# A new order of the first loads, transposes copied by one engine, and a new priority table in a one-core attention and FFN kernel

## Chip, cores, metric

One core of a Trainium2 chip. The metric is device time of one execution in microseconds (us). "Span" is the profiled length from the first to the last instruction, 1.7 to 1.8 us shorter than the time of the same execution.

## The reference

Layer norm of x (2048 x 512), then x plus two branches: a dilated sliding-window attention (32 heads of 16, window of 8 with step 2) and a gated FFN (512 to 1376 to 512).

```python
x = A_x
xn = _layernorm(x, axis=-1)
return x + _A_ref(xn, A_wqkv, A_wo) + _B_ref(xn, B_w_gate, B_w_up, B_w_down)
# _A_ref: qkv = xn @ wqkv; logits of q with k at pos, pos-2, ... pos-14; softmax; weighted v; @ wo
# _B_ref: (gelu(xn @ w_gate) * (xn @ w_up)) @ w_down
```

## The kernel before

The kernel builds a graph of several hundred tasks. A list scheduler inside the kernel file puts them in one fixed order per engine, from a priority per task, a table of shifts per group of tasks (SHIFT), and constants (SCHED: slack, tolerance). On the chip each engine executes its list strictly in that order, with semaphore waits.

The work goes in four blocks of 512 rows. At the start everything waits for memory, so the first block is done in four tiles of 128 rows: load, statistics, norm (VectorE, with the square root on ScalarE), four transposes on TensorE into PSUM, a copy to SBUF, then Q and K of this tile (16 matmuls of 128 columns each).

```python
# loads: all from the SyncE queue; lower priority value is issued first
prio=(-958, -957.5, -898)[i]                                    # Wq, Wk, Wv: 512 KiB (524 KB) each
prio=((-960, -959), (-957.8, -956.5))[p][t2]                    # tiles 0,1,2,3: 128 KiB (131 KB) each
# -> tile 0, tile 1, Wq, tile 2, Wk, tile 3, Wv

# first tile's transposes lie in two PSUM buffers: ScalarE copies one half, VectorE the other
it_t2 = Item("tpy" + nm, P_ps, "tp") if nm == "0_0" else it_tp
...
# fixed orders within engines
chain(["bnst0", "bnag0", "sub0", "rstd0", "norm0", "bnst1", "bnag1", "evy0_0", "sub1", "rstd1", "norm1",
       "bnst2", ... "norm3", "bnst4"])                           # VectorE; evy0_0 is its half copy
chain(... ["tpx0_0"] + ... + ["mmt0_0", "tpx0_1", "mmt1_0", "mmt0_1", "tpx1_0", "mmt1_1", "tpx1_1",
       "mmt0_2", "mmt1_2", "mmt0_3", "mmt1_3"])                  # TensorE; mmt0_t is Q, mmt1_t is K of tile t
```

After that comes the body: V of the first block, gate and up projections, logits and value products (VectorE multiplies, small TensorE reductions), softmax, later blocks' QKV, output tiles. The gate weight's load waits for Wk's landing; its issue is therefore a clock for that landing.

Of the kernel before, what the change touches and what calls it, by code (L numbers as in the profile page):

```python
# [11 lines left out]
    TOL=dict(pe=0.6, act=-0.3, dve=0.0, pool=0.0, sp=0.0),  # L12
    DMA_ISSUE=0.48,
    DMA_FIXED=2.0,
    DMA_BPUS=330e3,
    ACT_SWITCH=1.35,
    PE_SLACK=0.0,
# [128 lines left out]
class Graph:  # L146
# [466 lines left out]
    def report(self):  # L613
# [11 lines left out]


SHIFT = {
    "acc0": 361, "acc1": -284, "acc3": -893, "er1": 381, "er2": 159, "er3": -18, "ffn0": 449, "ffn1": -216,
    "ffn2": 73, "ffn3": -40, "fin0": -21, "fin1": 305, "fin2": 27, "fin3": -492, "h0": -6, "h1": -944,
    "h2": 606, "ldb1": 326, "ldb2": -35, "ln1": -1581, "ln2": 55, "prod0": 440, "prod1": 888, "prod3": -18,  # L630
    "pv1": -412, "pv2": 970, "pvr0": -976, "pvr1": 126, "pvr2": 463, "qkv1": -43, "qkv2": -1147, "qkv3": -216,
    "sm1": -57, "sm2": -519, "sm3": 750,
}
SCHED = dict(PE_SLACK=1.6, DMA_BPUS=250e3,
             TOL=dict(pe=0.6, act=-0.3, dve=-0.3, pool=-0.3, sp=0.0))

GROUPS = ((r"(?:bnst|bnag|ve|sq|rstd|sub|norm)(\d+)$", "ln", 4), (r"trx(\d+)", "ln", 2),
          (r"(?:mm|evq|evk|evv|stv)(\d)_", "qkv", 1), (r"pr(\d)_", "prod", 1), (r"er(\d)_", "er", 1),
# [21 lines left out]
def d_dve(n, rate=1.04):  # L660
    return 0.07 + n * rate * 1e-3
# [6 lines left out]
def bass_parallel_sum__sliding_local_dilated__glu_gated_geglu__prompt_kernel(nc, A_x, A_wqkv, A_wo, B_x, B_w_gate, B_w_up, B_w_down, out, dbg=None, cfg=None):  # L668
# [41 lines left out]
    with contextlib.ExitStack() as es:  # L710
# [11 lines left out]
        xnT = sb("xnT", [128, NXT, 4, 512], BF)  # L722
# [188 lines left out]
        for p in range(NP):  # L911
# [5 lines left out]
            if p < 2:  # L917
                for t2 in range(2):
                    def mk_ld(t2=t2, p=p, it=it_x):
                        return lambda e: e.dma_start(  # L920
                            XIN[:, it.slot, t2, :], x2[256 * p + 128 * t2:256 * p + 128 * t2 + 128, :])
                    t_x = G.task("sp", "ld_x%d_%d" % (p, t2), 0, mk_ld(), wr=[(it_x, t2)],
                                 prio=((-960, -959), (-957.8, -956.5))[p][t2], nbytes=128 * 1024)
            else:
                def mk_ld(p=p, it=it_x):
                    return lambda e: e.dma_start(
                        XIN[:, it.slot, :, :], x2[256 * p:256 * p + 256, :].rearrange("(t q) d -> q t d", q=128))
                t_x = G.task("sp", "ld_x%d" % p, 0, mk_ld(), wr=[(it_x, 0), (it_x, 1)],
                             prio=(0, 0, -897.5, -897)[p] if p < 4 else -950 + p * 20, nbytes=256 * 1024)
# [77 lines left out]
            for grp in ((0,), (1,)):  # L1007
                n = len(grp)
                nm = "%d_%d" % (p, grp[0])
                it_tp = Item("tpx" + nm, P_ps, "tp")  # L1010
                it_t2 = Item("tpy" + nm, P_ps, "tp") if nm == "0_0" else it_tp

                def mk_tp(it=it_tp, it2=it_t2, ito=it_x, grp=grp, n=n):
                    def f(e):
                        ins = None
                        for q, t2 in enumerate(grp):
                            for kt in range(4):
                                c0 = 1024 * (it, it2)[kt // 2].slot + kt * 128 * n + q * 128
                                ins = e.transpose(PSB[:, c0:c0 + 128], XIN[:, ito.slot, t2, kt * 128:(kt + 1) * 128],
                                                  ident[:, :])  # L1020
                        return ins
                    return f
                t_tp = G.task("pe", "tpx" + nm, d_mm(128, 4 * n), mk_tp(), rd=[(it_x, t2) for t2 in grp] + [I_ident],
                       wr=[it_tp] if it_t2 is it_tp else [it_tp, it_t2], prio=(-200 if b == 0 else base + 4), mode="f", util=0.5)

                t_tp.urgent = b == 0

                o = 256 * (p % 2) + 128 * grp[0]
                if p == 0 and grp[0] == 0:
                    def mk_ev2(it=it_t2, itx=XTI[b], o=o):  # L1030
                        return lambda e: e.tensor_copy(
                            out=xnT[:, itx.slot, 2:4, o:o + 128],
                            in_=PSB[:, 1024 * it.slot + 256:1024 * it.slot + 512].rearrange("q (k c) -> q k c", k=2))
                    t_of["evy" + nm] = G.task("dve", "evy" + nm, d_dve(256), mk_ev2(), rd=[it_t2],
                                              wr=[(XTI[b], ("y", p % 2, grp[0]))], prio=-200)
                nk = 2 if "evy" + nm in t_of else 4

                def mk_ev(it=it_tp, itx=XTI[b], n=n, o=o, nk=nk):
                    return lambda e: e.activation(
                        out=xnT[:, itx.slot, 0:nk, o:o + 128 * n],  # L1040
                        in_=PSB[:, 1024 * it.slot:1024 * it.slot + 128 * nk * n].rearrange("q (k c) -> q k c", k=nk),
                        func=ACTF.Identity)
                t_ev = G.task("act", "evx" + nm, d_act(128 * nk * n), mk_ev(), rd=[it_tp],
                              wr=[(XTI[b], (p % 2, t2)) for t2 in grp], prio=(-200 if b == 0 else base + 6))
                t_of["evx" + nm] = t_ev
                t_of["tpx" + nm] = t_tp
        def chain(names):
            ts = [t_of[q] if isinstance(q, str) else q for q in names]
            for q0, q1 in zip(ts, ts[1:]):
                G.order_after(q1, q0)  # L1050

        chain(["bnst0", "bnag0", "sub0", "rstd0", "norm0", "bnst1", "bnag1", "evy0_0", "sub1", "rstd1", "norm1",
               "bnst2", "bnag2", "sub2", "rstd2", "norm2", "bnst3", "bnag3", "sub3", "rstd3", "norm3", "bnst4"])
        chain(["norm3", "bnst5"])
        chain(["evx0_0", "sq1"])

        QTI = []
        for b in range(NB):
# [7 lines left out]
            if b == 0:  # L1066
                lead = []
                for t in range(4):
                    for which in range(2):
                        it_mm = Item("mmt%d_%d" % (which, t), P_ps, "qkv")  # L1070

                        def mk_mm(which=which, t=t, it=it_mm, itx=XTI[0]):
                            def f(e):
                                ins = None
                                for g in range(4):
                                    for kt in range(4):
                                        ins = e.matmul(  # L1077
                                            PS[:, 512 * it.slot + 128 * g:512 * it.slot + 128 * g + 128],
                                            lhsT=Wqkv[:, kt, which * 512 + g * 128:which * 512 + (g + 1) * 128],
                                            rhs=xnT[:, itx.slot, kt, t * 128:(t + 1) * 128],  # L1080
                                            start=(kt == 0), stop=(kt == 3))
                                return ins
                            return f
                        t_mm = G.task("pe", "mmt%d_%d" % (which, t), 16 * 0.0563, mk_mm(),
                                      rd=[(XTI[0], (t // 2, t % 2)), (I_wq, "qk"[which])]
                                      + ([(XTI[0], ("y", 0, 0))] if t == 0 else []), wr=[it_mm],
                                      prio=-100 + t, mode="f")
                        t_mm.urgent = True
                        t_of["mmt%d_%d" % (which, t)] = t_mm

                        def mk_e(which=which, t=t, it=it_mm, itq=it_qt):
                            def f(e):
                                if which == 0:
                                    o = QT[:, itq.slot, :, t * 128:(t + 1) * 128]
                                else:
                                    o = KT[:, KTI[0].slot, :, 16 + t * 128:16 + (t + 1) * 128]
                                return e.activation(
                                    out=o, in_=PS[:, 512 * it.slot:512 * it.slot + 512].rearrange(
                                        "q (g c) -> q g c", g=4), func=ACTF.Identity)
                            return f  # L1100
                        t_of["ev%s0_%d" % ("qk"[which], t)] = G.task("act", "ev%s0_%d" % ("qk"[which], t), d_act(512), mk_e(), rd=[it_mm],
                               wr=[(it_qt, ("t", t)) if which == 0 else (KTI[0], ("t", t))], prio=-100 + t)
                chain(["evk0_0", "sq3"])
                chain(warm_tasks[:len(WARM[0])] + ["tpx0_0"] + warm_tasks[len(WARM[0]):] +
                      ["mmt0_0", "tpx0_1", "mmt1_0", "mmt0_1", "tpx1_0", "mmt1_1", "tpx1_1",
                       "mmt0_2", "mmt1_2", "mmt0_3", "mmt1_3"])
            for hf in range(nh):
                xparts = [XTI[b]] if nh == 1 else [(XTI[b], (hf, 0)), (XTI[b], (hf, 1))]
                hb = base + (10 * hf if nh > 1 else 0)
# [414 lines left out]
```

## Time and profile before

| | before |
|---|---|
| median time | 196.71 us (3 runs), 196.53 with the run made beside the changed kernel |
| span of the profiled run | 194.6 us |
| TensorE busy | 97% |
| VectorE, ScalarE busy | 79%, 53% |
| first Q / first K matmuls begin; V begins | 6.04 / 7.83; 14.70 us |
| last matmul ends | 192.14 us |

The lines stand in the prediction below. The way to read them: a busy share of 97% says which engine sets the end, not that it is dense. So count matmuls by their spacing, and look for what is left. Three times are read from the chain of waits: where V begins (the end of the last K matmul; the prediction counts from the first V matmul in the chain, 0.05 us later), where the last matmul ends, and the difference. The first is "the start", the difference is "the body".

In the profile lines `PS` is a PSUM buffer, `XIN` a tile of x, `xnT` its transposed norm. L937 is a tile's statistics, L993 the end of its norm, L1019 its transposes on TensorE. The line numbers below differ by 6 or 7 between the kernels: L1077 before is L1071 in the changed kernel (Q and K of the first block), L1123 is L1116 (V, later Q, K, V), L1039 is L1032 (ScalarE's copy), L1308 is L1301 (value products on VectorE), L1329 is L1322 (their reductions on TensorE), L1360 is L1353 (gate and up), L1435 and L1439 are L1428 and L1432 (output tiles). In e5b L1077 is L1078.

### The profile page before, as it was taken

The page shows a single profiled execution, that of the slowest core. Times are in us where ns is not written, and L with a number is a line of the kernel's source. Part 1 is how long each engine was busy: PE and PEld are TensorE (multiplying, and loading weights), DVE is VectorE, ACT ScalarE, POOL GpSimd, SP SyncE. Part 2 cuts the span into 40 slices and gives each one's busy share as a digit, 9 for nine tenths or more (in the row PEclk, how much of TensorE's full clock was granted, in tenths as well). Part 3 has the DMA queues.
Part 4 walks back from the last instruction along what each step waited for, and adds up shares of the span by engine and source line. Part 5 has one row for each costly group of instructions (what it writes and reads, how often), then busy time and mean ns, then how long its engine had stood idle before and what let it go on. Part 6 is the DMA issues. An engine that isn't in the chain of part 4 may idle for free.

```text
span 194.6 us, 3228 instructions
## 1 busy us (share of the span) xinstructions
PE 188.5 (97%) x1205; PEld 91.1 (47%) x1224; DVE 153.6 (79%) x240; ACT 104.1 (53%) x171; POOL 8.5 (4%) x31
## 2 busy tenths in 40 slices
PE   7899999999999999999999999999999999999994
PEld 2794444444444443444434444444444444344484
DVE  5989978999799999998999866998974619972132
ACT  3577583776973679701457701764679006586000
POOL 6011001001000000001000100000000000000000
DMA  5999998998723853063657454014970440010121
GB/s 141 352 398 315 312 169 183 263 193 208 185 57 82 220 141 83 18 167 106 162 157 195 58 136 135 27 45 123 245 185 3 108 136 27 0 59 0 44 77 40
DMA packets 34799, 27.03 MB, mean 139 GB/s; under 512 B 11264, under 2 KB 33248, under 8 KB 34784
## 3 DMA queue, kind: packets, MB, share of 16 engines
q1 hardware_dynamic: 34784, 26.83, 54.1%
q8 instruction: 9, 0.15, 0.4%
q14 instruction: 6, 0.05, 0.1%
HBM read 19.99 MB, written 5.26 MB: 130 GB/s over the span
## 4 chain that ended last, share of the span: by engine, by line
PE 81%; DVE 8%; issue 3%; ACT 3%; DMA 3%; SPq 1%; DVEq 0%; ACTq 0%
PE PS L1360 29%; PE PS L1439 19%; PE PS L1123 13%; PE PS L1435 7%; DVE UNI L1308 4%; PE PS L1329 3%; PE PS L1077 3%; PE PS L1207 3%; DMA Wqkv<-in_A_wqkv_dram 3%; PE PS L1395 1%; DVE UNI L1177 1%; ACT UU L1377 1%; PE PS L1200 1%; DVE HT L1382 1%; DVE HT L1410 1%
## 5 line engine op out<-in xcount | busy, mean ns | idle before, releaser
L1439 PE MATMUL PS<-Wd,HT 128*128 128x512 bf16 (+2 forms) x205 | 40.8, 345 | 0.2
L1360 PE MATMUL PS<-xnT,Wu 128*128 128x512 bf16 x154 | 39.6, 379 | 0.6 <-issue 0.5
L1360 PE MATMUL PS<-xnT,Wg 128*128 128x512 bf16 x156 | 39.4, 379 | 0.4 <-issue 0.3
L1308 DVE TENSOR_TENSOR UNI<-BS,PT 128x2048 bf16<-128x2048 bf16 x32 | 37.1, 1219 | 2.9 <-DMA XR<-in_A_x_dram 1.8
L1177 DVE TENSOR_TENSOR UNI<-QT,KT 128x2048 bf16<-128x2048 bf16 x32 | 37.1, 1218 | 0.2
L1377 ACT ACTIVATE UU<-PS 128x512 bf16<-128x512 f32 x40 | 24.0, 601 | 21.2 <-PE PS L1360 21.1
L1123 PE MATMUL PS<-xnT,Wqkv 128*128 128x512 bf16 x155 | 34.8, 379 | 0.5 <-DVE PS L1245 0.2
L1370 ACT ACTIVATE GG<-PS 128x512 bf16<-128x512 f32 x40 | 23.8, 602 | 18.2 <-PE PS L1360 18.1
L1439 PEld LDWEIGHTS PS<-Wd,HT 128*128 128x128 bf16 x209 | 19.6, 98 | 18.5
L1459 DVE TENSOR_TENSOR OB<-PS,XR 128x512 bf16<-128x512 f32 (+2 forms) x19 | 11.5, 605 | 18.3 <-PE PS L1439 18.3
L1360 PEld LDWEIGHTS PS<-xnT,Wg 128*128 128x128 bf16 x160 | 15.3, 98 | 19.6 <-ACT UU L1377 0.8
L1360 PEld LDWEIGHTS PS<-xnT,Wu 128*128 128x128 bf16 x160 | 15.3, 98 | 19.6 <-issue 0.8
L1123 PEld LDWEIGHTS PS<-xnT,Wqkv 128*128 128x128 bf16 x160 | 15.4, 98 | 19.2 <-issue 0.8
L1382 DVE TENSOR_TENSOR HT<-GG,UU 128x512 bf16<-128x512 bf16 x40 | 15.8, 421 | 9.5 <-ACT UU L1377 9.4
L1435 PE MATMUL PS<-Wo,OT 128*128 128x512 bf16 (+2 forms) x76 | 16.9, 345 | 0.1
L1133 ACT ACTIVATE QT<-PS 128x512 bf16<-128x512 f32 x12 | 7.2, 597 | 15.4 <-PE PS L1123 15.4
L1340 ACT ACTIVATE OT<-PS 128x512 bf16<-128x512 f32 x16 | 8.7, 594 | 5.9 <-PE PS L1329 5.8
L1147 ACT ACTIVATE VT<-PS 128x512 bf16<-128x512 f32 x16 | 9.6, 597 | 4.1 <-PE PS L1123 4.1
L937 DVE BATCH_NORM_STATS2 st<-XIN 128x6 f32<-128x512 bf16 x16 | 10.4, 682 | 1.2 <-DMA XIN<-in_A_x_dram 1.2
L1435 PEld LDWEIGHTS PS<-Wo,OT 128*128 128x128 bf16 x76 | 7.2, 98 | 7.0
L1140 ACT ACTIVATE KT<-PS 128x512 bf16<-128x512 f32 x12 | 7.2, 598 | 2.9 <-PE PS L1123 2.9
L1077 PE MATMUL PS<-xnT,Wqkv 128*128 128x128 bf16 x128 | 7.8, 219 | 0.6 <-DMA Wqkv<-in_A_wqkv_dram 0.5
(63 smaller groups left out, 130.9 us busy)
## 6 DMA issues: line engine op xcount, KB each, us to landing
BS<-vt_scratch SPq DMA_DIRECT2D x64, 128.5 KB, 3.0
vt_scratch<-VT SPq DMA_DIRECT2D x16, 128.0 KB
XR<-in_A_x_dram SPq DMA_DIRECT2D x16, 128.0 KB, 2.1
out_dram<-OB SPq DMA_DIRECT2D x14, 128.0 KB, 2.0
Wqkv<-in_A_wqkv_dram SPq DMA_DIRECT2D x3, 512.0 KB, 4.2
XIN<-in_A_x_dram SPq DMA_DIRECT2D x6, 256.0 KB, 7.9
Wg<-in_B_w_gate_dram SPq DMA_DIRECT2D x1, 1280.0 KB
Wu<-in_B_w_up_dram SPq DMA_DIRECT2D x1, 1280.0 KB
```

The costliest lines, as they stand in the source:

```text
L937: return lambda e: e.bn_stats(out=st[:, t, :], in_=XIN[:, it.slot, t2, :])
L1077: ins = e.matmul(PS[:, 512 * it.slot + 128 * g:512 * it.slot + 128 * g + 128], lhsT=Wqkv[:, kt, which * 512 + g * 128:which * 512 + (g + 1 ...
L1123: ins = e.matmul(PS[:, 512 * it.slot:512 * it.slot + HWD], lhsT=lhsT, rhs=xnT[:, itx.slot, kt, c0:c0 + HWD], start=(kt == 0), stop=(kt == 3))
L1177: return lambda e: e.tensor_tensor(out=UNI[:, it.slot, :, :], in0=bass.AP(QT, (itq.slot * 4 + g) * 512, [[NQT * 4 * 512, 128], [0, 4], [1, ...
L1308: return lambda e: e.tensor_tensor(out=bass.AP(UNI, ito.slot * 2048, [[NUNI * 2048, 128], [512, 4], [128, 4], [1, 128]]), in0=bass.AP(BS, ...
L1360: ins = e.matmul(PS[0:M, 512 * it.slot:512 * it.slot + 512], lhsT=Wx[:, kt, j * 128:j * 128 + M], rhs=xnT[:, itx.slot, kt, :], start=(kt = ...
L1370: return lambda e: e.activation(out=GG[0:M, ito.slot, :], in_=PS[0:M, 512 * it.slot:512 * it.slot + 512], func=ACTF.Gelu_apprx_tanh)
L1377: return lambda e: e.activation(out=UU[0:M, ito.slot, :], in_=PS[0:M, 512 * it.slot:512 * it.slot + 512], func=ACTF.Identity)
L1382: return lambda e: e.tensor_tensor(out=HT[0:M, ito.slot, j, :], in0=GG[0:M, ig.slot, :], in1=UU[0:M, iu.slot, :], op=ALU.mult)
L1435: ins = e.matmul(PS[:, 512 * it.slot:512 * it.slot + CW], lhsT=OT[:, ito.slot, dq, ti * 128:(ti + 1) * 128], rhs=Wo[:, dq, c0:c1], start=( ...
L1439: ins = e.matmul(PS[:, 512 * it.slot:512 * it.slot + CW], lhsT=HT[:, ith.slot, j, ti * 128:(ti + 1) * 128], rhs=Wd[:, j, c0:c1], start=Fal ...
L1459: return lambda e: e.tensor_tensor(out=OB[:, ito.slot, 0:CW], in0=PS[:, 512 * it.slot:512 * it.slot + CW], in1=XR[:, itx.slot, c0:c1], op= ...
```

## The change

Its intent: get Wq and Wk sooner, since TensorE waits for Wk; take VectorE's half copy out, so that the first Q does not depend on VectorE; let the third tile's Q run while the fourth tile is still being normed; and search the priority table again for this start.

```diff
-                 prio=((-960, -959), (-957.8, -956.5))[p][t2]     # tile 0, tile 1, Wq, tile 2, Wk, tile 3
+                 prio=((-960, -957.9), (-957.2, -956.5))[p][t2]   # tile 0, Wq, tile 1, Wk, tile 2, tile 3
-                it_t2 = Item("tpy" + nm, P_ps, "tp") if nm == "0_0" else it_tp
+                it_t2 = it_tp
-                if p == 0 and grp[0] == 0:      # ... VectorE's copy evy0_0, removed
-        chain([... "bnst1", "bnag1", "evy0_0", "sub1", ...])
-        chain(["norm3", "bnst5"])
-        chain(["evx0_0", "sq1"])
+        chain([... "bnst1", "bnag1", "sub1", ...])
+        for q in ("bnst5", "bnst6", "bnst7"):
+            chain(["norm3", q])
+        chain(["evx0_0", "sq1", "evx0_1", "sq2"])
-                chain(["evk0_0", "sq3"])
+                chain(["evx1_0", "sq3"])
-                 "mmt1_1", "tpx1_1", "mmt0_2",
+                 "mmt1_1", "mmt0_2", "tpx1_1",
-SHIFT = { ... 35 entries ... }
-SCHED = dict(PE_SLACK=1.6, ..., TOL=dict(pe=0.6, ...))
+SHIFT = { ... 35 other entries ... }
+SCHED = dict(PE_SLACK=1.0, ..., TOL=dict(pe=0.3, ...))
```

## The prediction

> **What bounds the kernel now.** I read the page first (busy shares, chain), then the pieces of the chain, TensorE's waits, the first 16 us of the timeline, and the busy table by stage.
>
> ```profile
> PE 188.5 (97%) x1205; PEld 91.1 (47%) x1224; DVE 153.6 (79%) x240; ACT 104.1 (53%) x171; POOL 8.5 (4%) x31
> ...
> PE 81%; DVE 8%; issue 3%; ACT 3%; DMA 3%; SPq 1%; DVEq 0%; ACTq 0%
> ```
>
> TensorE (PE) is busy 97% of the span; no other engine is near. A busy share can hide stalls, so I count the work instead. In the chain of waits:
>
> ```profile
> 2.73 5.05 DMA Wqkv<-in_A_wqkv_dram
> 7.78 0.05 issue
> 7.83 1.96 PE PS L1077 x32
> 9.79 0.22 PE PS L1019 x4
> 10.01 0.89 PE PS L1077 x16
> 10.90 0.22 PE PS L1019 x4
> 11.13 3.57 PE PS L1077 x64
> 14.70 0.05 issue
> 14.75 3.40 PE PS L1123 x15
> ...
> 119.78 6.91 PE PS L1123 x32
> ...
> 192.23 0.29 DVE OB L1459
> ```
>
> (The columns are start, length, what.) 32 full-width matmuls in 6.91 us are 216 ns each; 64 of 128 columns in 3.57 us are 55.8 ns each. Between 14.75 (first V matmul) and 185.54 (the split last tiles), the kernel has 706 full-width matmuls: 16 for the first block's V, 144 for Q, K, V of three blocks, 320 for gate and up, 16 for their last slice, 210 for 14 output tiles of 15. 706 x 0.216 = 152.5 us. Four logit reductions at 0.56 + 1.84 and eight value reductions at 0.98 add 9.6 + 7.8. Together 169.9 of a stretch of 170.8 us. So some 0.9 us of TensorE time is lost in the whole body; it runs dense, although 12 of those us on the chain pass through VectorE.
>
> TensorE's complete list of waits says the same:
>
> ```profile
> PE PS L863 <- DVE wsrc L812: 1.2, 1, 1.2
> PE PS L1360 <- issue: 0.8, 5, 0.2
> PE PS L1077 <- DMA Wqkv<-in_A_wqkv_dram: 0.5, 1, 0.5
> PE PS L1123 <- DVE PS L1245: 0.2, 1, 0.2
> PE PS L1123 <- issue: 0.2, 1, 0.2
> ```
>
> The third line is what the change is after: the first K projection waits for Wk. The start itself, in the timeline:
>
> ```profile
> 5.50 0.38 ACT L1039 ACTIVATE xnT<-PS 128x256 bf16<-128x256 bf16 x1 [1.34 <-PE PS L1019]
> 5.53 0.26 DVE L1031 COPY xnT<-PS 128x256 bf16<-128x256 bf16 x1
> 6.04 1.05 PE L1077 MATMUL PS<-xnT,Wqkv 128*128 128x128 bf16 x16
> 7.71 0.58 ACT L1039 ACTIVATE xnT<-PS 128x512 bf16<-128x512 bf16 x1
> 7.83 1.96 PE L1077 MATMUL PS<-xnT,Wqkv 128*128 128x128 bf16 x32 [0.51 <-DMA Wqkv<-in_A_wqkv_dram]
> ```
>
> The first Q projection starts at 6.04, 0.16 us after ScalarE's half copy; then the fourth item in the load queue's way, Wk, holds TensorE until 7.83.
>
> **What the Trainium skill says.** "TensorE: Matmul & The Clock Gate", section "Wait - 56ns, not 53.3ns?", gives 55.6 and 215.7 ns from start to start at 128 and 512 columns with the clock released; the trace has 55.8 and 216, and a granted clock of 1.00 in every stage. "DMA: Bandwidth & Descriptors", section "Queues, rings and completion order", says that one issuing queue's descriptors are consumed in ring order on each DMA engine; so what is issued ahead of Wk delays it. The trace fits: Wk, issued fifth, landed at 7.78, and the order of bytes below accounts for it. "ScalarE: Activation LUTs", section "What ACT_TABLE_LOAD costs", gives 186 ns + 0.833 ns per element: 0.40 us at 256, 0.61 at 512; the trace has 0.38 and 0.58. The first-named page, section "Architectural detail", calls ScalarE and VectorE strict FIFO: an early instruction that waits blocks ready ones behind it. The trace has such a place: the transposes of the second tile had begun at 6.93, but the third tile's square root went first on ScalarE (7.51), and the copy started only at 7.71.
>
> **The change, part by part.**
> Loads. Before: tile 0, tile 1, Wq, tile 2, Wk, tile 3. After: tile 0, Wq, tile 1, Wk, tile 2, tile 3. A tile is 131 KB, a weight third 524 KB. The busy table, whose last column is GB/s:
>
> ```profile
> 1.50:3.00 1.50, 1.50 (x5) 0.51 (x4) 0.56 (x2) 0.78 (x2) 1.30 (x10) 1.00 0.57 180
> 3.00:4.00 1.00, 1.00 (x4) 0.37 (x3) 0.93 (x3) 0.13 (x1) 0.78 (x5) 1.00 0.71 111
> 4.00:5.00 1.00, 1.00 (x5) 0.29 (x4) 0.96 (x4) 0.17 (x1) 0.50 (x3) 1.00 1.02 350
> 5.00:6.00 1.00, 0.93 (x6) 0.41 (x4) 0.97 (x4) 0.50 (x2) 0.00 (x0) 1.00 1.09 384
> 6.00:7.00 1.00, 0.96 (x18) 0.99 (x19) 0.92 (x4) 0.07 (x1) 0.00 (x0) 1.00 1.09 342
> ```
>
> Summed: 270 KB by 3.0 (tiles 0 and 1), 381 by 4.0, 731 by 5.0, 1115 by 6.0, 1457 by 7.0. The bytes up to Wq (786 KB) are through at 5.14, up to Wk (1442 KB) at 6.96; Wk was seen 0.82 later. The dip at 3 to 4 us is Wq's start: it was issued at 1.71. After, it is issued in second place (1.26, 0.45 earlier), so the dip and all that follows should come up to 0.45 earlier, and Wk has one tile less ahead (131 KB at 384 GB/s, 0.34). Estimate: bytes of Wk through at 6.96 - 0.45 - 0.34 = 6.2, seen at 7.0. Wk no longer binds. The price: tile 1 now follows Wq. Its bytes are through at 5.14 - 0.45 = 4.7 and with the 0.82 it is usable at 5.5, where before VectorE took it at 4.73. Tile 2 follows Wk by 131 KB / 342 = 0.38, usable at 7.4 instead of by 6.57.
>
> The copy. ScalarE copies all four transposes: 0.58 for 0.38, +0.2 us on the path to the first Q (6.24 instead of 6.04). VectorE loses one copy of 0.26 us.
>
> The walk. Tile 1's statistics to its norm took 4.73 to 6.65, 1.92 us with VectorE's copy in it, some 1.7 without: 5.5 + 1.7 = 7.2. Tile 0 shows 0.06 from norm to transpose: transposes at 7.26, after the first Q ends (6.24 + 0.89 = 7.13). They take 0.22, so the first K starts at 7.5 where it was 7.83. Second tile's Q: its copy ends about 7.7 + 0.6 = 8.3, before the K ends at 8.4. Third tile: norm at 7.4 + 1.82 (6.57 to 8.39 before) = 9.2, and TensorE arrives at 7.5 + 2 x 0.89 = 9.3. Fourth: norm at 9.2 + 1.85 = 11.1; TensorE, which now does the third tile's Q before these transposes, arrives at 9.3 + 0.22 + 1.78 = 11.3. No wait, by a margin of 0.1 to 0.2. From the first K, TensorE has 7 x 0.89 + 2 x 0.22 = 6.7 us plus 0.2 of gaps: V starts at 14.4 for 14.75. Gain 0.35 us.
>
> The rest. New priorities, less slack in the schedule for TensorE (1.0 for 1.6) and a smaller tolerance reorder the whole body, with the same instructions. Against 0.9 us of lost time there is next to nothing to win; a bad order could add waits. I take zero. The split output tiles (185.54 to 192.14) and the last add and store (to 194.6) keep their work. Sum: 196.7 - 0.35 = 196.35; I say 196.3.
>
> **The rivals.**
> One: tile 1 takes Wk's place as the wait. If Wq's data does not come earlier with its issue, tile 1 is usable at 5.96, its norm is done at 7.65, the first K starts at 7.9, and third and fourth tile follow as late: gain 0 or -0.2 us, time 196.7 to 196.9. For it: tile 2 and tile 3 fit by a tenth. Against: bytes were low from 3 to 4 us because little had been issued, not because the engines were full (share 0.71).
> Two: the reordered body decides. The chain from 53.8 to 72.5 us runs through VectorE, whose busy time there is 19.5 of 20; TensorE had only 0.2 us of wait, so the order covered it just so. With less slack, a few waits of 0.2 to 0.5 us each would cost 0.5 to 1.5 us: 197 to 198. Against: these constants look re-searched for this start, and the same search left 0.9 us before.
> Three: body gaps shrink too: at most 0.9 + 0.35, so 195.5. The five 0.16 us gaps stand beside the small reductions, which remain; I expect little.
>
> **Range and chances.** Between rival three and a mild rival two: 195.4 to 197.4. Faster by 2% means 3.9 us, over the 0.35 of the start plus all 0.9 of the body: 1%. Slower by 2% needs nearly 4 us of new waits: 4%. Within: 95%.
>
> **What would show each step.** First Q at about 6.25 and a 0.58 us copy of 512 columns in front of it, no copy on VectorE. The 0.5 us wait for Wk gone; first K at about 7.5, V's first matmul at about 14.4. Gate's load, which waited for Wk, issued at 7.0 instead of 7.8. Tile 1's statistics starting at 5.5, after an idle wait for its load. Matmuls at 216 ns between there and the tail, TensorE's waits in the body still under 1 us. I am wrong if a wait for the tiles, or for VectorE after 20 us, shows among TensorE's waits with more than 0.5 us, or if the start wins and the end does not move.

## The result, and the profile after

| | before | changed |
|---|---|---|
| median time | 196.53 us (4 runs, 196.06 to 196.84) | 196.62 us (4 runs, 196.51 to 196.87) |
| ratio, 95% interval | | 1.0008 (0.9984 to 1.0033) |
| span of the profiled run | 194.6 | 194.9 |
| V begins | 14.70 | 14.95 |
| last matmul ends | 192.14 | 192.51 |
| V to last matmul | 177.44 | 177.56 |

A ratio is the mean time of one kernel's fast runs over the mean of the other's fast runs of the same rounds, so it is not quite the ratio of the medians quoted beside it. Here the time is the same: the interval spans half a microsecond either way. The traces resolve more. Of the 0.37 us by which the last matmul ends later in this pair, 0.25 lies ahead of V and 0.12 in the body. The chain's lines for this (start, length, what) are, before and then changed:

```profile
11.13 3.57 PE PS L1077 x64
191.51 0.63 PE PS L1439 x11
```

```profile
12.27 2.68 PE PS L1071 x48
191.88 0.63 PE PS L1432 x11
```

First, the page's busy line and TensorE's waits of the changed kernel (us in total, times, longest).

```profile
PE 189.0 (97%) x1205; PEld 91.0 (47%) x1224; DVE 153.0 (78%) x239; ACT 104.3 (54%) x171; POOL 10.5 (5%) x31
```

```profile
PE PS L863 <- DVE wsrc L812: 1.2, 1, 1.2
PE PS L1353 <- issue: 0.6, 4, 0.2
PE PS L1019 <- DVE XIN L993: 0.6, 1, 0.6
PE PS L1388 <- issue: 0.2, 1, 0.2
PE PS L1071 <- ACT xnT L1032: 0.2, 1, 0.2
```

The wait for Wk (0.5 us) is gone. In its place stands one of 0.6 us: the second tile's transposes wait for its norm. Why the norm is late is in the timeline of the changed kernel:

```profile
5.51 0.60 ACT L1032 ACTIVATE xnT<-PS 128x512 bf16<-128x512 bf16 x1 [1.29 <-PE PS L1019]
5.97 0.69 DVE L937 BATCH_NORM_STATS2 st<-XIN 128x6 f32<-128x512 bf16 x1 [1.16 <-DMA XIN<-in_A_x_dram]
...
7.85 0.40 PE L1019 MATMUL PS<-ident,XIN 128*128 128x128 bf16 x4 [0.56 <-DVE XIN L993]
...
8.09 1.95 PE L1071 MATMUL PS<-xnT,Wqkv 128*128 128x128 bf16 x32
```

VectorE sat 1.16 us until the second tile's load landed (5.97; before the change it took this tile at 4.73 without a wait). So the first K starts at 8.09 and not at 7.83, although Wk had landed by 7.46 (the gate load's issue).

Then the load stream, in the busy table by stage (first column the stretch in us, then the busy time of TensorE, its weight loads, VectorE, ScalarE and GpSimd; the last three are the granted clock, the share of the DMA engines and GB/s). Before:

```profile
2.00:2.50 0.50, 0.50 (x2) 0.15 (x1) 0.00 (x0) 0.28 (x2) 0.41 (x2) 1.00 0.77 260
2.50:3.00 0.50, 0.50 (x3) 0.22 (x2) 0.08 (x1) 0.00 (x0) 0.46 (x4) 1.00 0.82 232
3.00:3.50 0.50, 0.50 (x3) 0.22 (x2) 0.50 (x1) 0.00 (x0) 0.36 (x2) 1.00 0.82 80
3.50:4.00 0.50, 0.50 (x3) 0.15 (x2) 0.43 (x3) 0.13 (x1) 0.42 (x3) 1.00 0.60 141
4.00:5.00 1.00, 1.00 (x5) 0.29 (x4) 0.96 (x4) 0.17 (x1) 0.50 (x3) 1.00 1.02 350
```

Changed:

```profile
2.00:2.50 0.50, 0.50 (x2) 0.15 (x1) 0.00 (x0) 0.28 (x2) 0.40 (x2) 1.00 1.18 260
2.50:3.00 0.50, 0.50 (x3) 0.22 (x2) 0.02 (x1) 0.00 (x0) 0.47 (x4) 1.00 0.75 70
3.00:3.50 0.50, 0.50 (x3) 0.22 (x2) 0.50 (x1) 0.00 (x0) 0.35 (x2) 1.00 0.81 150
3.50:4.00 0.50, 0.50 (x3) 0.16 (x2) 0.43 (x3) 0.07 (x1) 0.43 (x3) 1.00 0.83 266
4.00:5.00 1.00, 1.00 (x5) 0.29 (x4) 0.77 (x3) 0.23 (x1) 0.49 (x3) 1.00 1.09 385
```

Multiply rate by length: from 2.0 to 5.0 us 706 KB went through before, 758 KB after (with the 24 and 13 KB ahead of 2.0: 730 and 771). Moving Wq's issue 0.45 us forward bought 41 KB, which at 385 GB/s is 0.1 us. The other runs agree: by 5.0 us 702 to 735 KB were through in the five with the old start of the queue (before, e2, e4, e5b, e10) and 748 to 794 in the five with the new one (changed, e1, e3, e13, e14), 53 KB apart in the mean. The dip did move forward with Wq (70 GB/s already at 2.5 instead of 80 at 3.0), but before, by the sums, most of the second tile's 131 KB passed in the stretch from 2.5 to 3.0 (116 KB), while Wq was starting up. After, the second tile is queued behind Wq, and that stretch carries next to nothing.

### The profile page after: what moved, and what is told of

Its sections match the earlier page's. It is cut to its first block, busy times and chain, and to the rows that moved or that the text cites. A ratio compares the mean times of both kernels' runs of the same rounds, so it can differ in the third digit from the quotient of the medians.

```text
span 194.9 us, 3223 instructions
## 1 busy us (share of the span) xinstructions
PE 189.0 (97%) x1205; PEld 91.0 (47%) x1224; DVE 153.0 (78%) x239; ACT 104.3 (54%) x171; POOL 10.5 (5%) x31
## 4 chain that ended last, share of the span: by engine, by line
PE 94%; DMA 2%; DVE 1%; issue 1%; SPq 0%; DVEq 0%
PE PS L1353 35%; PE PS L1432 20%; PE PS L1116 18%; PE PS L1428 7%; PE PS L1322 4%; PE PS L1200 4%; PE PS L1071 3%; DMA XIN<-in_A_x_dram 2%; PE PS L1388 2%; PE PS L1193 1%; PE PS L1019 0%; DVE st L937 0%; SPq L872 0%; SPq L920 0%; DVE XIN L993 0%
## 5 line engine op out<-in xcount | busy, mean ns | idle before, releaser
L1353 PE MATMUL PS<-xnT,Wu 128*128 128x512 bf16 x157 | 40.3, 380 | 0.3 <-issue 0.2
L1116 PE MATMUL PS<-xnT,Wqkv 128*128 128x512 bf16 x157 | 35.8, 379 | 0.2
L1116 PEld LDWEIGHTS PS<-xnT,Wqkv 128*128 128x128 bf16 x160 | 15.6, 98 | 18.7
L1375 DVE TENSOR_TENSOR HT<-GG,UU 128x512 bf16<-128x512 bf16 x40 | 15.9, 421 | 7.6 <-ACT UU L1370 6.9
```

The costliest lines, as they stand in the source:

```text
L1116: ins = e.matmul(PS[:, 512 * it.slot:512 * it.slot + HWD], lhsT=lhsT, rhs=xnT[:, itx.slot, kt, c0:c0 + HWD], start=(kt == 0), stop=(kt == 3))
L1353: ins = e.matmul(PS[0:M, 512 * it.slot:512 * it.slot + 512], lhsT=Wx[:, kt, j * 128:j * 128 + M], rhs=xnT[:, itx.slot, kt, :], start=(kt = ...
L1375: return lambda e: e.tensor_tensor(out=HT[0:M, ito.slot, j, :], in0=GG[0:M, ig.slot, :], in1=UU[0:M, iu.slot, :], op=ALU.mult)
```

## The experiments

Twelve kernels were run, all correct against the reference. The table collects what their traces show; the sections tell why each was made. V and last matmul are read from each chain of waits; "gate issued" is the clock for Wk's landing. Old loads means tile 0, tile 1, Wq, tile 2, Wk; new loads tile 0, Wq, tile 1, Wk.

| run | tile 1 taken | gate issued | first K | V | V to last matmul | median (before beside it) | ratio |
|---|---|---|---|---|---|---|---|
| before | 4.73 | 7.80 | 7.83 | 14.70 | 177.44 | 196.53 | |
| changed | 5.97 | 7.46 | 8.09 | 14.95 | 177.56 | 196.62 (196.53) | 1.0008 |
| e1_loads_only | 5.75 | 7.25 | 8.05 | 15.38 | 177.45 | 197.01 (196.38) | 1.0036 |
| e2_old_loads | 4.71 | 8.52 | 8.55 | 15.42 | 177.56 | 197.03 (196.38) | 1.0015 |
| e4_body_only | 4.79 | 8.01 | 8.04 | 14.91 | 177.56 | 196.84 (196.38) | 1.0013 |
| e6_wq_act | 5.57 | 7.08 | 7.69 | 14.55 | 177.56 | 196.50 (196.38) | 0.9991 |
| e7_touch | 6.23 | 7.69 | 8.35 | 15.21 | 177.56 | 197.02 (196.41) | 1.0012 |
| e8_tile1_act | 5.44 | 7.45 | 8.01 | 14.87 | 177.56 | 196.49 (196.41) | 0.9992 |
| e3_start_only | 5.81 | 7.30 | 7.93 | 14.79 | 182.15 | 201.07 (196.41) | 1.0221 |
| e9_tile1_act2 | 6.17 | 8.20 | 8.28 | 15.15 | 177.55 | 196.86 (196.53) | 1.0018 |
| e10_wk_before_2 | 4.72 | 7.35 | 7.50 | 14.71 | 177.55 | 196.62 (196.53) | 1.0010 |
| e13_old_shift | 5.80 | 7.31 | 7.92 | 14.78 | 185.10 | 204.50 (196.53) | 1.0407 |
| e14_old_sched | 5.84 | 7.34 | 7.96 | 14.82 | 177.44 | 196.53 (196.53) | 1.0003 |
| e5b_copy_guard | 4.75 | 8.05 | 8.08 | 14.95 | 182.90 | 202.03 (196.48) | 1.0288 |

The 95% intervals of the ratios that are within 1% of 1 are 0.2 to 0.6% wide to either side, and all of them hold 1. Only the three large ratios are differences that the times themselves show (e3's interval, 1.0165 to 1.0277, leaves out 1 but reaches below 1.02, so its size against 2% is unclear); the rest is read from the traces, one execution each.

### e1: the new loads alone

Before, with the new load priorities. The three compute engines' instruction lists are those of before, line for line.

```diff
-prio=((-960, -959), (-957.8, -956.5))[p][t2]
+prio=((-960, -957.9), (-957.2, -956.5))[p][t2]
```

> The kernel before with only the new order of loads; the instruction order of TensorE, ScalarE and VectorE is that of before, line for line. Theory (the second tile became the wait): its statistics start at about 6.0 instead of 4.73, as in the changed kernel. VectorE's copy of the first transposes stands behind those statistics in VectorE's fixed order, so it moves from 5.53 to about 6.9 and the first Q projection from 6.04 to about 7.2; on ScalarE the third tile's square root stands ahead of the second tile's copy, which then ends near 9.9. The V projection starts at about 15.9 instead of 14.75, the time is about 197.6 us (ratio 1.005 to 1.006). Rival (Wk's earlier landing decides, the rest is slack): V starts at 14.4, time 0.3 us below before.

The direction came out, at a little over half the size: V at 15.38 (0.68 after before's, 1.15 expected). The timeline of e1 shows both couplings:

```profile
5.75 0.69 DVE L937 BATCH_NORM_STATS2 st<-XIN 128x6 f32<-128x512 bf16 x1 [0.93 <-DMA XIN<-in_A_x_dram]
6.57 0.26 DVE L1031 COPY xnT<-PS 128x256 bf16<-128x256 bf16 x1
...
6.93 1.05 PE L1077 MATMUL PS<-xnT,Wqkv 128*128 128x128 bf16 x16 [1.39 <-DVE xnT L1031]
...
8.57 0.30 ACT L951 ACTIVATE sq<-mv,eps 128x1 bf16<-128x1 bf16 x1 [1.58 <-DVE mv L941]
8.77 0.58 ACT L1039 ACTIVATE xnT<-PS 128x512 bf16<-128x512 bf16 x1
```

The first tile's copy on VectorE (6.57) stands in the list behind the second tile's statistics, so the first Q now waits 1.39 us for work on another tile; and on ScalarE the copy for the second tile waits behind a square root that is not ready. This fits the change taking VectorE's copy out and fixing ScalarE's order: V is at 15.38 without the two, at 14.78 to 14.95 with them and the same loads. I had expected V at 15.9; the second tile came 0.25 us sooner than I took, and VectorE's copy began before the aggregate had quite ended.

### e2 and e4: the old loads under the changed kernel, and the new table under the kernel before

```diff
 e2 (from changed): -((-960, -957.9), (-957.2, -956.5))   +((-960, -959), (-957.8, -956.5))
 e4 (from before):  SHIFT, SCHED of the changed kernel
```

> The changed kernel with only the old order of loads; the instruction order of the three compute engines is that of the changed kernel, line for line. Theory (the second tile became the wait): its statistics start at 4.7 again, the first Q stays at about 6.15 (ScalarE's 0.6 us copy stays), Wk holds the first K until about 7.8, the V projection starts at about 14.7, some 0.3 us earlier than the 15.00 of the changed kernel, and the end comes 0.3 us earlier too; time 196.3 us, ratio to before 0.998 to 1.000. Rival (the reordered body sets the end): the end stays where the changed kernel has it, 192.5, whatever the start does.

> The kernel before with only the new priorities and the new scheduling constants; the start is unchanged. Theory (the body is dense in both orders): V starts at 14.75 and the stretch from there to the split last tiles is 170.8 to 171.0 us, as in both kernels; time within 0.1 us of before, ratio 0.999 to 1.001. Rival (the new order adds waits): a stretch of 171.3 us or more and TensorE waits over 1 us in the body.

In e2 the second tile was taken at 4.71 as expected, but V did not come earlier: 15.42. In this execution Wq itself landed late (the first Q waited for it until 6.75) and Wk at 8.52, with the same loads issued at the same times as in before, to 0.01 us. So the expectation of a V at 14.7 fell, through something I had not allowed for: the same six loads land up to 0.7 us apart from one execution to the next (gate issued at 7.80, 8.52, 8.01 and 8.05 in before, e2, e4 and e5b). The rival of e2 (the end stays where it was) fell too: its end moved with V. e4's body came out as expected: 177.56, which is 0.12 more than with the old table and constants. Its ratio, 1.0013, is just outside the expected 0.999 to 1.001, well inside its interval.

Read down the column "V to last matmul": 177.44 and 177.45 for the list of before with V at 14.70 and 15.38; 177.55 or 177.56 for the list of the changed kernel with V anywhere between 14.55 and 15.42. The body is rigid. Whatever the start wins or loses arrives at the end in full, and the new table and constants together cost 0.12 us. (e14 below has the new table with the old constants, and 177.44: so it is the constants that cost them, not the table.)

### e6, e7, e8, e9: what slows the stream at its start

Each is the changed kernel's compute order (line for line on TensorE and VectorE, on ScalarE but for the loads it issues).

```diff
 e6: Wq issued from ScalarE's queue at 0.80; the other loads keep their sequence
 e7: a load of 8 KB of Wqkv into an unused buffer from ScalarE's queue, ahead of everything
 e8: old sequence of loads, but tile 1 issued from ScalarE's queue at 0.79
 e9: as e8, with e7's small load ahead of tile 1 on ScalarE's queue
```

> The changed kernel with Wq's load issued from ScalarE's queue at the very start, so that it no longer stands in the one issuing line: tile 0 and tile 1 are issued at 0.8 and 1.26, Wk at about 1.7 instead of 2.27. Theory A (the slow start of the loads follows each load's issue): everything comes about 0.5 us earlier, the second tile's statistics start at about 5.2 instead of 5.97, the first K at about 7.3 instead of 8.25, V at about 14.3. Theory B (the stream is slow until about 3.75 us whatever is issued): the second tile shares the stream with Wq and its statistics still start at 5.7 to 6.0, V at 14.8 to 15.0. In time A is 0.6 us less than the changed kernel, B the same.

> The changed kernel with one small extra load (64 pieces of 128 bytes out of the QKV weight, into a buffer nobody reads) issued from ScalarE's queue at 0.8 us, ahead of everything; the compute engines' order is that of the changed kernel. In all six traces so far the load stream falls to 30 to 150 GB/s for about 0.8 us when the first weight load starts. Theory T1 (the first reads of the weight tensor are slow, whoever makes them): the slow stretch moves ahead or vanishes, 480 KB or more instead of 386 KB are through at 4.0 us, the second tile's statistics start at about 5.4 instead of 5.97, V at about 14.4. Theory T2 (the slow stretch belongs to the big weight load itself, its start-up from its own issue): nothing moves, 380 KB at 4.0, second tile at 5.8 to 6.0, V at 14.9 to 15.0.

> The changed kernel's compute order with the old sequence of loads, the second tile issued from ScalarE's queue at 0.8 beside the first (so Wq is issued at 1.26, as in the changed kernel, but with nothing behind it that the first tiles need). If the account of the start is right (a weight load takes about 2.1 us from its issue to full rate, and only loads that are already in front can use that time): both tiles are through by 3.0, the second tile's statistics follow the first tile's norm at 4.75, about 440 KB or more are through at 4.0 and 820 KB at 5.0 instead of 731, Wk lands at about 7.4 (before: 7.78), first K at 7.5, V at 14.3 to 14.4, time 0.4 us under before or a little more. Rival (the engines stall on the weight's first reads whichever queue they come from, as with Wq on ScalarE's queue): the second tile is held up as well and lands after 5.3, V at 14.6 or later.

> The changed kernel's compute order; first tile, Wq, third tile, Wk, fourth tile from the usual queue, the second tile from ScalarE's queue behind one small unused load, so issued at about 1.25 instead of 0.8. The run with the second tile at 0.8 gained on Wk (7.44) but lost 0.7 us on the first tile, with which it shared the stream. If sharing was the cost: first tile's statistics at 3.0 to 3.2 again, the second tile's at 4.8 to 5.2, first K at 7.5, V's first full matmul at 14.2 to 14.5. Rival (Wq's slow start holds up every load that is in flight with it): second tile at 5.4 or later, V at 14.6 to 15.0.

The load stream of e6:

```profile
2.50:3.00 0.50, 0.50 (x3) 0.22 (x2) 0.00 (x0) 0.27 (x2) 0.47 (x4) 1.00 0.44 68
3.00:3.50 0.50, 0.50 (x3) 0.23 (x2) 0.41 (x1) 0.00 (x0) 0.35 (x2) 1.00 0.78 250
3.50:4.00 0.50, 0.50 (x3) 0.16 (x2) 0.46 (x2) 0.00 (x0) 0.43 (x3) 1.00 1.05 362
```

With Wq issued 0.46 us earlier than in the changed kernel the stream is at full rate from 3.5 on, not from about 4.0. In before, changed and e6 Wq's issue ended at 2.14, 1.68 and 1.26, and the stream stood above 370 GB/s from 4.25, 4.0 and 3.5: 2.1 to 2.3 us after the issue had ended. In quarters of a microsecond, and with 340 GB/s as the mark, all five runs with the old start of the queue get there at 4.25 and the five with the new one between 3.5 and 4.0: 1.8 to 2.3 us after the end of Wq's issue. That is theory A. But tile 1, issued at 1.26 on the other queue, was usable only at 5.57 (A said 5.2), and V came at 14.55 (A said 14.3): a little over half of A's gain, in one execution.

e7 fits neither the fast case of T1 nor quite T2: 411 KB were through at 4.0 (T1 wanted 480, T2 380), and the tile landed late, at 6.23. Reading a few rows of the weight ahead did not remove the slow stretch.

e8 brought the stream forward as expected (503 KB at 4.0, 874 at 5.0) and Wk with it, but the two first tiles were issued side by side on two queues, and the first was taken at 3.70 instead of 2.98, which fits their sharing the stream; the first Q started at 6.88, and V at 14.87. It traded one wait for another. e9 meant to repair that by issuing tile 1 half a microsecond later, and its rival won: the first tile was taken at 3.24, but tile 1 only at 6.17, and V came at 15.15, later even than the rival's 15.0. In e6 and e9 tile 1 was in flight beside the starting weight load, and came late in both although another queue carried it. That the slow weight pieces hold up whatever is on the same DMA engines fits all four runs; no run isolates it (e9 also carries e7's small load, with which tile 1 came at 6.23 on the usual queue too), and what makes the start of a weight load slow stays open.

### e10: a third order of loads

```diff
-((-960, -957.9), (-957.2, -956.5))     +((-960, -959), (-957.2, -956.5))   # tiles 0, 1, Wq, Wk, tiles 2, 3
```

> The changed kernel with a third order of loads: first, second tile, Wq, Wk, third, fourth tile; same compute order. If every order of the same bytes through one queue only moves the wait: the second tile's statistics at 4.75, Wk at 7.2 to 8.0 (a third of a microsecond before what the old order gives, less its spread of 0.7 us), but the third tile now lands behind it, its statistics at 7.6 to 8.3 instead of 6.6, and TensorE waits for the third tile's transposes; V's first matmul again at 14.5 to 15.3. Rival (there is a good order, and neither kernel has it): V at 14.2 or earlier.

As expected. The first K starts at 7.50, earliest of all, and the third tile takes the place of the wait. The third tile's statistics in e10:

```profile
7.73 0.69 DVE L937 BATCH_NORM_STATS2 st<-XIN 128x6 f32<-128x512 bf16 x1 [0.87 <-DMA XIN<-in_A_x_dram]
```

Before the change this tile was taken at 6.57 without a wait. TensorE waits 0.2 us for its transposes, and V begins at 14.71, within 0.01 us of before.

### e3, e13, e14, e5b: the priority table

```diff
 e3  (from changed): SHIFT and SCHED of before (table and constants)
 e13 (from changed): SHIFT of before only
 e14 (from changed): SCHED of before only (slack 1.6, tolerance 0.6)
 e5b (from before):  VectorE's copy removed, ScalarE copies all four transposes, and the guard
                     "norm3 before bnst5, bnst6, bnst7"; old loads, old TensorE sequence, old table and constants
```

> The changed kernel with the old priorities and scheduling constants: the new start with a body ordered by the old constants. By the theory the start is that of the changed kernel within the spread of the loads (second tile's statistics at 5.7 to 6.0, V at 14.8 to 15.0) and the stretch from V to the split last tiles is 170.8 to 171.0 us whichever constants order it; time within 0.3 us of the changed kernel. Rival (the new constants were needed by the new start): the body is longer by 0.5 us or more, with TensorE waits on ScalarE or VectorE in it.

> The changed kernel with the old table of priority shifts, but the new slack and tolerance. The old table and old constants together under the new start cost 4.6 us, all of it after 126 us, where TensorE waits for value products and output copies. If the table is what has to fit the start: the same kind of loss, 1 to 5 us, with waits of TensorE on VectorE or ScalarE after 120 us. Rival (slack and tolerance did it): the body is 170.8 to 171.2 us, time as the changed kernel.

> The changed kernel with the new table of priority shifts but the old slack (1.6) and tolerance (0.6). If the table is what has to fit: little is lost, body 170.9 to 171.5 us, time within 0.5 us of the changed kernel. Rival (slack and tolerance did it): 1 to 5 us lost, late waits on VectorE or ScalarE.

> The kernel before, its loads, its TensorE start sequence, its table and constants all kept; only VectorE's copy of the first transposes goes to ScalarE, and the guard is added that keeps the second block's statistics behind the fourth tile's norm. The start: first Q at about 6.2 instead of 6.04, then Wk's landing holds the first K as before (7.8 to 8.5), so V within the spread 14.7 to 15.4: the copy by itself costs nothing. The question is the body. If the old table is fitted so closely that any change of the start's task list breaks it: TensorE waits on VectorE or ScalarE after 120 us, V to last matmul 179 to 186 us instead of 177.4, time 198 to 205. Rival (the table was broken by the new sequence of TensorE at the start, not by the copy): V to last matmul 177.4 to 178, time within 0.5 us of before.

Here my theory fell. I had taken the body for dense under either table. With the new start and the old table and constants (e3) the kernel loses 4.7 us (201.07 against 196.41), and its body is 4.6 us longer than the changed kernel's. TensorE's waits in e3, the two largest:

```profile
PE PS L1322 <- DVE UNI L1301: 2.3, 2, 1.5
PE PS L1428 <- ACT OT L1333: 1.7, 2, 1.2
```

and in e13, where the waits for VectorE's value products are longest:

```profile
PE PS L1322 <- DVE UNI L1301: 5.7, 2, 3.6
```

e13 and e14 separate the two parts. The table is what has to fit: with the old one and the new slack the loss is 8.0 us, more than the 1 to 5 expected; with the new one and the old slack the body is 177.44, the best there is, and the time that of before. In e13 the granted clock fell as well: 0.89 in the stage from 120 to 150 us, 0.983 over the span, where the kernels without such waits have 0.999 or 1.000; all four executions of e13 have it (0.975 to 0.983), so how much of the 8.0 us is the clock stays open. In e3 the clock is not the cause: its profiled run has the loss at 1.000. The profiled run of e5b shows 0.97 from 120 to 180 us, but its two executions at 1.000 over the span (202.06, 202.81) were no faster than the two at 0.991 (202.01, 201.72).

e5b shows how little it takes. It keeps everything of before except who copies one half tile, and the guard; and it costs 5.5 us (202.03 against 196.48). The guard by itself leaves every engine's instruction list as it was (built, not run), so it is the copy. The guard is needed because without it, in another build that was not run, two statistics of the second block, with the work on them, move ahead of the end of the fourth tile's norm, which would then wait for their load. The start of e5b is within the spread (V at 14.95). TensorE's waits in e5b:

```profile
PE PS L1329 <- DVE HT L1410: 2.2, 1, 2.2
PE PS L863 <- DVE wsrc L812: 1.2, 1, 1.2
PE PS L1078 <- DMA Wqkv<-in_A_wqkv_dram: 1.2, 2, 0.7
PE PS L1435 <- ACT OT L1340: 1.2, 1, 1.2
```

The two waits after 120 us, for VectorE (2.2) and ScalarE (1.2), are 3.4 of the 5.5 us; the rest is not placed. The old table fits one task list. With one task fewer the scheduler's choices fall out differently (in builds of both, 87 of the 182 places on TensorE's list differ), and after 120 us VectorE and ScalarE no longer deliver in time. The new SHIFT table undoes that, and this is most of what the change's tuning does.

No kernel here is shown to be faster than before. The best start (e6, V at 14.55) and the best body (e14, 177.44) together would end some 0.15 us ahead of before's profiled run; the narrowest interval above is 0.19% to either side, 0.37 us, so it could not be told from before and was not run.

## Why the prediction was right or wrong

The time (196.62 for 196.3) and the class are right, and the range holds it. That is no proof of the account: a gain of 0.35 us and none lie in the same range. The small gain is not there, and the step that failed is in the start. The prediction's own sign of being wrong, a wait for the tiles of more than 0.5 us, did show: TensorE waits 0.6 us for the second tile's norm.

**The stream of loads.** "The dip and all that follows should come up to 0.45 earlier" is the term that was mis-sized: 0.1 us instead of 0.45. The prediction put the low rate from 3 to 4 us down to little having been issued; but Wq's 524 KB had been issued by 2.14. The slow stretch goes with the start of a weight load (full rate 1.8 to 2.3 us after the end of its issue, in eleven runs), and before the change the second tile's bytes filled part of it. By the prediction's own sums the 786 KB up to tile 1 were through at 5.04 where it had 4.7 (5.14 before). So tile 1 was usable at 5.97 instead of 5.5 (5.75 to 5.97 in the five runs with the new sequence on one queue) and Wk at 7.46 instead of 7.0. A second term was small by 0.12: statistics to norm took 1.82 us, not 1.7 (the prediction has this 1.82 itself, for the third tile, which had no copy in it). Together 0.47 + 0.12: the first K came at 8.09 instead of 7.5. This is the first rival of the prediction, nearly to the number: it put tile 1 at 5.96, the first K at 7.9 and the time at 196.7 to 196.9 (measured 5.97, 8.09, 196.62).

**The copy.** Right. The first Q started at 6.16 (I said 6.24), behind a 0.60 us copy of 512 columns. It costs nothing that counts, since the wait behind it is longer.

**The third and fourth tile.** Right: no wait for either in the changed kernel; the third tile's statistics (7.84) follow the second's norm at once. Statistics to norm of the fourth tile take 2.08 us (1.99 before, not the 1.85 of the prediction); it was done at 11.66, and TensorE, itself 0.6 us later than predicted, came at 11.88.

**V.** In the prediction's count the first V matmul is at 15.00 instead of 14.4, and 14.75 before: from the first K on the walk took 6.91 us for the 6.9 predicted. But "before" was one look. Four executions with the old loads have V at 14.70, 14.91, 14.95 and 15.42; four with the new loads and ScalarE's copy at 14.78, 14.79, 14.82 and 14.95. The means are 15.00 and 14.84. The profile from which I predicted was the luckiest of its four. What the order does is clearer one step earlier, where the two sets of four do not overlap: the gate load's issue came at 8.10 in the mean with the old loads and at 7.35 with the new ones, and the second tile was taken at 4.75 and 5.86. Wk did gain about what was forecast (0.74 for 0.8); the second tile paid more than was forecast (1.1 for 0.8), and it then held TensorE. The new start may be 0.15 us better and steadier, but the two sets overlap, and e2 and e5b have other compute orders than before; it is not shown.

**The body.** "I take zero": 0.12 us longer, right in size; e14 lays the 0.12 on the slack and tolerance. "The same search left 0.9 us before" was an argument for it; e3, e13 and e5b show what it rests on. Zero is not what the new start does to the body by itself (4.6 us longer); it is what is left after the new table has repaired it. The prediction named the alternative in its second rival (new waits on VectorE with a reordered body), sized it at 0.5 to 1.5 us, and was right that it would not show. Where a table does not fit, as in e3, e13 and e5b, the body is 4.6 to 7.5 us longer, three times the rival's size or more. Two readings there were off without effect: VectorE has 16 us, not 12, on the chain before the tail, and "19.5 of 20" is the stretch from 60 to 80 us (from 53.8 to 72.5 it is 18.4 of 18.7). Wk stands fifth in the queue, as the prediction says in one place, not fourth, as in another.

So the expected gain went in two steps: the wait for Wk became a wait for the second tile, and the reordered body gave back another tenth, which is the constants' part. Against a spread of 0.7 us in the landing of the same loads, neither is seen in the time.

## What to carry to other kernels

Where several loads share one stream and all are needed soon, a new order moves the wait from one consumer to the next; before reordering, write down when each load is needed, and whether small loads fill the time in which a large one starts up. Take the same start from several executions before spending a term of a few tenths on it. And in a kernel whose order comes from a tuned table, a change of one task is never local: keep the engines' instruction lists equal while testing (as e1, e2, e6 to e10 do), or the table's loss of 5 us is booked to the wrong cause.

## What the Trainium skill lacked or had wrong

- "DMA: Bandwidth & Descriptors", section "Latency and other measured facts", gives about 0.6 us to the first byte for this kind of queue; here the first bytes moved between 1.75 and 2.00 us, 0.55 to 0.8 us after the end of the first issue, so this agrees. No page has the slow stretch that followed: with a 512 KiB weight load (1 KiB pieces) in the queue the stream reached full rate only 2.1 to 2.3 us after the end of that load's issue, with 68 to 266 GB/s in the half microseconds between 2.5 and full rate (before, changed, e6; 1.0 to 1.5 us of it).
- No page has the spread of landing: loads issued at the same times, to 0.01 us for Wq and Wk, in before, e2, e4 and e5b had Wk landed at 7.80, 8.52, 8.01 and 8.05 us by the gate load's issue.
- "TensorE: Matmul & The Clock Gate", section "Back-to-back issue gap", gives about 131 ns per matmul of 512 columns as a sustained rate in a stream of weight loads and matmuls, which is too low for this kernel. Here 32 of them took 6.91 us, 216 ns each, with weight loads in between; the same page's formula (N / 2.4 + 2.5 ns) fits.
